# Two gates begun instead of one, weights in two parts, a new hand-written order for the second half, and other places for the third half's attention pieces

## The chip, the core and the metric

The kernel runs on one core of one Trainium2 chip. The metric is device time in microseconds (us) of one execution; the median of several runs counts. The engines are named as in the profile: PE (TensorE, matrix products), PEld (its weight loads), DVE (VectorE), ACT (ScalarE), POOL (GpSimd, which also issues the loads that change type on the way), SP (SyncE, which issues the other transfers).

## The reference

Attention with a sliding window and a few global keys, then a gated feed-forward layer:

```python
# q, k, v: (4 batches, 8 heads, 768 tokens, 64); n_global = 8, n_local = 96
scores = scale * q @ k.T                        # per batch and head
keep = (key < n_global) | ((0 <= rel) & (rel < n_local))      # rel = query - key
dist = n_local where a key is global and not local, else |rel|
scores = where(keep, scores - slope[head] * dist, -1e9)
a = softmax(scores); x = a @ v                  # -> (3072 tokens, 512)
gate = maximum(x @ w_gate, 0); val = x @ w_val  # 512 -> 1536
out = (gate * val) @ w_out                      # 1536 -> 512, float32
```

## The kernel before

The 4 x 768 tokens are cut into 8 halves of 384 tokens, numbered 0 to 7. For each half there is attention (four head pairs p = 0 to 3) and a feed-forward part. Feed-forward for half c is made of pieces: for each of 12 column blocks fc a gate piece (four products of 128x128 weights with 128x384 of xT, then a relu on ACT) and a val piece (four products, then a multiplication with the relu's result on DVE), and after that the output pieces. The four products of a piece run over the four chunks of xT, and chunk p of xT is what the normalisation of head pair p writes. Output rows n = 0, 1 are made by a seven-product scheme (m1 to m7, `winograd`) that needs sums of ht and of w_out blocks on DVE (`add`, L535; `wo_sum`), the rest by plain pieces (`outp`).

All engines run their instructions in the order in which the program was written out. That order is hand-made:

- The first half's attention runs alone. Meanwhile POOL issues loads in this order: v of half 0, the first weight group (wg[0] and wv[0], blocks fc 0 to 3), then q and k of half 1 (`kq1`, heads 4 to 7 first, then heads 0 to 3), v rows of half 1, the second weight group (fc 4 to 7).
- The second half's stage then interleaves half 1's attention with fc 0 to 7 of half 0's feed-forward. Its order is a string of short names (L802): g and v are a gate or val piece, K the transposes of q and k of a head pair, S its scores with masks (S31 is pair 3, group 1), A its sums and values, N its normalisation, m a mask built on ACT. Just before the string runs `begin()`, which starts gate 0 and val 0 with the first three of their four chunks, so that `g0` and `v0` in the string only add the last chunk. PSUM has two `ff` banks for feed-forward pieces here, two score tiles (`s`) of two banks each and two `t` banks. The piece K0 also issues q and k loads of half 2 on SP, the piece S20 the third weight group, w_out and pad fills on POOL.
- From then on `weave` mixes feed-forward pieces with attention pieces of the next half: each attention piece gets a place, a share of the stage's total weight (`spread` puts a list evenly between two shares), and is written out once the feed-forward pieces before it reach that share. PSUM now has three `ff` banks and five `x` banks. For half 2 (the third) the stage is fc 8 to 11 of halves 0 and 1 followed by their output pieces, 39 pieces of equal weight; the attention pieces of half 2 come from `attention_pieces(2)`, in which `gap` is an empty place. Its scores take four x banks for a pair, the values one for each head, and the norm (`piece_norm`, L446) frees the latter.
- At the end of that stage stood the last norm of half 2, after all other pieces. Half 2's own feed-forward then started with `begin()`, which there also begins gate 1.
- `held` (L842) is a one-element copy on POOL that reads w_out; behind it stand the last cast and the three transposing transfers for half 2's keys and queries.

Of the kernel before, what the change touches and what calls it, by code (L numbers as in the profile page):

```python
# [8 lines left out]
FP32 = mybir.dt.float32  # L9
# [6 lines left out]
def kernel(  # L16
# [19 lines left out]
    N_DC = DM // 128  # L36
# [38 lines left out]
    psum = {}  # L75
# [17 lines left out]
    GW = 4  # L93
# [399 lines left out]
    def attention_pieces(s):  # L493
        QK = lambda p: [(0.15, lambda g=g: piece_qk(s, p, g)) for g in range(3)]
        AV = lambda p: [(0.29, lambda e=e: piece_av(s, p, e)) for e in range(2)]
        N = lambda p: [(0.0, lambda: piece_norm(s, p))]
        g = QK(3)
        a = AV(2)
        gap = [(0.0, lambda: None)]
        return (QK(0) + QK(1) + AV(0) + N(0) + gap + QK(2) + AV(1) + N(1) + gap  # L500
                + g[0:1] + a[0:1] + g[1:2] + a[1:2] + g[2:3] + N(2) + AV(3) + N(3))

# [95 lines left out]
    def ffn_pieces(c):  # L598
        ht = ht_pool.tile([128, N_FC, QH], BF16, name="ht")
        st = {}  # L600

        def product(w, key, fc, d0, d1):
            key = key, fc
            if d0 == 0:
                st[key] = psum["ff"].tile([128, 512], FP32, name="ff_ps")
            for dc in range(d0, d1):
                nc.tensor.matmul(st[key][:, 0:QH], lhsT=w_of(w, dc, fc), rhs=xT_of[c][:, dc, :],  # L607
                                 start=(dc == 0), stop=(dc == N_DC - 1))

        def gate(fc, d0=0):  # L610
            product(wg, "g", fc, d0, N_DC)
            psg = st["g", fc]
            gr = gr_pool.tile([128, QH], BF16, name="grelu")
            nc.scalar.activation(gr, psg[:, 0:QH], AF.Relu, bias=0.0, scale=1.0)  # L614
            st["gr", fc] = gr

        def val(fc, d0=0):
            product(wv, "v", fc, d0, N_DC)
            psv = st["v", fc]
            nc.vector.tensor_tensor(ht[:, fc, :], psv[:, 0:QH], st["gr", fc], op=ALU.mult)  # L620

        def outp(n, part):
            if part == 0:
                st["o"] = psum["ff"].tile([128, 512], FP32, name="ff_ps")
            ps2 = st["o"]
            for fc in range(part * N_FC // 4, (part + 1) * N_FC // 4):
                nc.tensor.matmul(ps2, lhsT=ht[:, fc, n * 128 : (n + 1) * 128],  # L627
                                 rhs=wo_sb[:, fc, :],
                                 start=(fc == 0), stop=(fc == N_FC - 1))
            if part == 3:  # L630
                osb = late["osb"].tile([128, DM], FP32, name="osb")
                nc.scalar.copy(osb, ps2)
                nc.sync.dma_start(out=out_v[c, n], in_=osb)

        def begin():
            for d0, d1 in ((0, 2), (2, N_DC - 1)):
                product(wg, "g", 0, d0, d1)
                product(wv, "v", 0, d0, d1)
            if c == 2:
                product(wg, "g", 1, 0, N_DC - 1)  # L640

        plain = range(NN) if c < 1 else () if c - c % 2 in PAIRED else (NN - 1,)
        add, products = winograd([(c, ht, 0), (c, ht, 1)], "sums", (1, 5, 6, 4, 7, 2, 3) if c == NHALF - 1 else
                                 (1, 2, 5, 6, 4, 3, 7) if c in PAIRED else (1, 5, 4, 6, 2, 3, 7))
        behind = {2: [lambda: add(3, 0, 3)], 5: [lambda: add(3, 3, 6)], 8: [lambda: add(1, 0, 3)],
                  9: [lambda: add(2, 0, 3)], 10: [lambda: add(4, 0, 3)]}
        rest = tuple(lambda j=j: add(j, 3, 6) for j in (1, 2, 4))
        if c in PAIRED:
            third_of[c] = ht
        elif c - 1 in PAIRED:  # L650
            add3, products3 = winograd([(c, ht, NN - 1), (c - 1, third_of[c - 1], NN - 1)], "sums3",
                                       (1, 5, 4, 6, 2, 3, 7))
            behind.update({1: [lambda: add3(1)], 6: [lambda: add3(2)], 7: [lambda: add3(3)]})
            rest = (lambda: add3(4),) + rest

        def val_and_sums(fc):
            val(fc)
            for f in behind.get(fc, ()):
                f()

        begin_of[c] = (begin, lambda: gate(0, N_DC - 1), lambda: val(0, N_DC - 1))
        f1 = []
        for fc in range(N_FC):
            f1.append((0.65, lambda fc=fc: gate(fc)))
            f1.append((0.65, lambda fc=fc: (val if c < 1 else val_and_sums)(fc)))
        f2 = [(0.65, lambda n=n, part=part: outp(n, part))
              for n in plain for part in range(4)]
        if c == 2:
            f1[:2] = [(1.5, begin_of[c][0]), (0.15, begin_of[c][1]), (0.15, begin_of[c][2])]
            f1[3] = (0.15, lambda: gate(1, N_DC - 1))  # L670
        if c >= 1:
            f2 += (products3 if c - 1 in PAIRED else []) + products
            places = (2, 3, 5) if plain else (0, 1, 2) if c in PAIRED else (0, 1, 2, 3)
            for at, f in list(zip(places, rest))[::-1]:
                f2.insert(at, (0.0, f))
        return f1, f2
# [44 lines left out]
    scores(0, 0, 0)  # L721
    first_keys(1, A)
    nc.gpsimd.tensor_copy(hold[1], kT[0][1][0:1, 0, 0:1])
    load_w(wg[0], moe_w_gate, 0, GW * 128)
    load_w(wv[0], moe_w_val, 0, GW * 128)
    make_sel(1)
    make_sel(2)
    scores(0, 0, 1)
# [5 lines left out]
    for h0 in (4, 0):  # L734
        for i, src in enumerate((k, q)):
            nc.gpsimd.dma_start(out=kq1[:, i, h0 : h0 + 4, :], in_=rows_of(src, 1, h0, h0 + 4))
    nc.gpsimd.memset(vbuf[0][:, NT - 1, :].bitcast(mybir.dt.uint32), 0)
    for p in range(HP):
        nc.gpsimd.memset(kT[0][p][:, 6, NG + 48 : 128].bitcast(mybir.dt.uint32), 0)
# [39 lines left out]
    stack = open_psum(ff=2, s=2, t=2)  # L779
    f1_0, f2_0 = ffn_pieces(0)  # L780
    f1_1, f2_1 = ffn_pieces(1)
    g_of = [begin_of[0][1]] + [f for _, f in f1_0[2::2]]
    v_of = [begin_of[0][2]] + [f for _, f in f1_0[3::2]]
    K = [lambda p=p: second_keys(p) for p in range(HP)]

    def Z():
# [12 lines left out]

    more = {"K0": lambda: load_qk_after(2), "S20": loads}  # L800
    begin_of[0][0]()
    for f in ("m1 g0 m3 v0 m2 g1 K3 K2 m0 g3 K1 S30 S31 g2 K0 S20 v3 S11 v1 S21 A3 N3 v2 S00 S01 "  # L802
              "g5 A2 S10 g4 g6 A0 N2 v5 v4 N0 A1 N1 g7 v7 v6").split():
        i = int(f[1])
        if f[0] == "S":
            SC(i, int(f[2]))
# [35 lines left out]
    for f in (*casts[:7], lambda: nc.gpsimd.tensor_copy(held, wo_sb[0:1, N_FC - 1, 0:1]),  # L842
# [3 lines left out]
    load_v_half(3)  # L846
    weave(f1_1[G[0]])
    weave(f1_1[G[1]], [(0.1 + 0.12 * j, lambda j=j: fill_ones(nc.vector, 0, j)) for j in range(NT)])
    pieces = spread(attention_pieces(2), 0.375, 0.9)

    weave(f1_0[G[2]] + f1_1[G[2]] + f2_0 + f2_1 + [(0.0, pieces.pop()[1])],
          [(0.33, order_k[2]), (0.38, order_k[3])],
          pieces, spread(early_pieces(3), 0.58, 0.88),
          spread([(0.0, lambda j=j, part=part: wo_sum(j, part)) for j in (1, 3, 2, 4) for part in range(2)],
                 0.1, 0.74))

# [55 lines left out]
```

## Time and profile before

| | |
|---|---|
| median of 3 runs | 240.94 us (240.68 to 241.03) |
| profiled execution, its own time | 241.08 us |
| its span in the profile | 239.3 us |
| granted PE clock | 1.0 |
| PE busy | 232.4 us, 97% of the span |
| DVE, ACT, POOL busy | 172.3, 156.4, 86.0 us |

The span runs from the first to the last instruction of the program; 1.8 us of the execution lie around it. In the profile's lines, L607 is a product of a gate or val piece, L614 the relu, L620 the multiplication, L272 the transposes of K, L341 the scores S, L459 the sums and values A of the second half, L397 and L427 the scores and values of later halves, L436 and L441 the logarithm and exponential that make a reciprocal, L446 the norm, L549 the seven-product scheme. A timeline line has start, length, engine, line, operation, out<-in, shapes, count, and in brackets the idle time before it and what ended it. Products are pipelined: a product of 384 columns is listed with 0.32 us, though the next one can start after about half of that.

### The profile page before, as it was taken

What the parts mean: (1) busy time and instruction counts of PE and PEld (TensorE: products, weight loads), DVE (VectorE), ACT (ScalarE), POOL (GpSimd) and SP (SyncE); (2) the same over time, 40 slices, a digit from 0 to 9 for tenths busy, and PEclk for the clock granted to TensorE, in tenths of its full rate; (3) what the DMA queues carried; (4) which work ended last, traced back from release to release, by engine and by line L of the source; (5) the groups of instructions that cost most, each with busy time, mean ns of one, the idle gap of its engine ahead of it and who ended that gap; (6) DMA issues with size and microseconds to landing.
All of it is one profiled execution on the core that took longest, in us unless ns stands there. A gap on an engine that the chain in (4) does not pass through costs nothing.

```text
span 239.3 us, 5430 instructions
## 1 busy us (share of the span) xinstructions
PE 232.4 (97%) x1977; PEld 150.2 (63%) x1981; DVE 172.3 (72%) x456; ACT 156.4 (65%) x358; POOL 86.0 (36%) x202
## 2 busy tenths in 40 slices
PE   7999999999999999999999999999999999999994
PEld 3655555665458456676657666766678666766683
DVE  7775955858665788756787686967986786955752
ACT  5897883337776677757877578657786678634331
POOL 6776894207323952702357042723350000000000
PEclk9999999999999999999999999999999999999999
DMA  6999999994947997469439966197432200020022
GB/s 208 179 197 177 257 243 213 184 162 96 272 137 135 287 173 126 31 140 277 77 58 79 223 199 114 22 174 230 77 58 88 90 0 0 4 88 0 3 76 101
DMA packets 69460, 31.42 MB, mean 131 GB/s; under 512 B 47145, under 2 KB 66345, under 8 KB 69433
## 3 DMA queue, kind: packets, MB, share of 16 engines
q0 software_dynamic: 31744, 8.71, 35.6%
q1 hardware_dynamic: 36472, 21.45, 34.4%
q10 hardware_dynamic: 1216, 0.92, 1.2%
q8 instruction: 15, 0.25, 0.4%
q14 instruction: 13, 0.10, 0.1%
HBM read 28.41 MB, written 6.29 MB: 145 GB/s over the span
## 4 chain that ended last, share of the span: by engine, by line
PE 92%; DVE 3%; ACT 2%; DMA 1%; issue 0%
PE ff_ps L607 52%; PE ff_ps L549 12%; PE x_ps L427 6%; PE ff_ps L627 6%; PE x_ps L549 5%; PE x_ps L397 4%; PE t_ps L459 2%; PE s_ps L341 2%; PE t_ps L272 2%; DMA kq<-in_k_dram 1%; PE t_ps L310 1%; DVE xT L446 1%; ACT lnd L436 1%; PE s_ps L321 1%; ACT ef L347 0%
## 5 line engine op out<-in xcount | busy, mean ns | idle before, releaser
L607 PE MATMUL ff_ps<-xT,wg 128*128 128x384 bf16 x384 | 79.0, 326 | 0.8 <-ACT grelu L614 0.4
L607 PE MATMUL ff_ps<-xT,wv 128*128 128x384 bf16 x384 | 78.6, 326 | 0.0
L614 ACT ACTIVATE grelu<-ff_ps 128x384 bf16<-128x384 f32 x96 | 46.9, 490 | 46.6 <-PE ff_ps L607 24.5
L620 DVE TENSOR_TENSOR ht<-ff_ps,grelu 128x384 bf16<-128x384 f32 x96 | 53.2, 555 | 29.1 <-PE ff_ps L607 18.5
L607 PEld LDWEIGHTS <-wg 128*128 128x128 bf16 x384 | 36.1, 98 | 23.5 <-issue 1.0
L607 PEld LDWEIGHTS <-wv 128*128 128x128 bf16 x384 | 35.7, 98 | 23.9 <-issue 1.2
L406 ACT ACTIVATE es<-x_ps 128x360 bf16<-128x360 f32 (+2 forms) x96 | 35.8, 447 | 3.1 <-PE x_ps L397 3.0
L359 DVE TENSOR_TENSOR es<-es,m_all 128x432 bf16<-128x432 bf16 (+4 forms) x108 | 30.0, 328 | 6.0 <-ACT es L406 5.9
L446 DVE TENSOR_TENSOR xT<-x_ps,rcp 64x384 bf16<-64x384 f32 x48 | 26.6, 554 | 7.5 <-ACT rcp L441 6.8
L436 ACT ACTIVATE lnd<-x_ps 64x384 f32<-64x384 f32 x48 | 23.3, 485 | 11.3 <-PE x_ps L427 10.6
L363 POOL CAST kqc<-ks 128x384 bf16<-128x384 f32 x24 | 11.2, 514 | 33.0 <-DMA ks<-in_k_dram 33.0
L549 PEld LDWEIGHTS <-s 128*128 128x128 bf16 x216 | 21.1, 98 | 2.4
L137 POOL DMA_DIRECT2D vbuf<-in_v_dram x25 | 21.6, 876 | 1.1 <-DMA wv<-in_moe_w_val_dram 0.8
L427 PE MATMUL x_ps<-es,vbuf 128*128 128x216 bf16 (+4 forms) x216 | 21.8, 225 | 0.0
L549 PE MATMUL ff_ps<-t,s 128*128 128x256 bf16 x162 | 21.6, 273 | 0.0
L427 PEld LDWEIGHTS <-vbuf 128*128 128x128 bf16 x216 | 15.8, 97 | 6.8
L627 PE MATMUL ff_ps<-wo_sb,ht 128*128 128x512 bf16 x68 | 17.8, 379 | 0.2
L549 PEld LDWEIGHTS <-ht 128*128 128x128 bf16 x162 | 15.5, 98 | 2.5 <-DVE xT L446 0.2
L263 POOL COPY kT<-kqT 128x240 bf16<-128x240 bf16 x16 | 6.9, 431 | 23.5 <-DMA kqT<-kqc 20.7
L363 POOL CAST kqc<-qs 128x384 bf16<-128x384 f32 x24 | 12.1, 543 | 8.3 <-DMA qs<-in_q_dram 8.3
L535 DVE TENSOR_TENSOR s<-ht 128x384 bf16<-128x384 bf16 (+1 forms) x32 | 13.3, 416 | 0.9
L441 ACT ACTIVATE rcp<-lnd 128x384 f32<-128x384 f32 x24 | 12.6, 524 | 0.8
(114 smaller groups left out, 241.2 us busy)
## 6 DMA issues: line engine op xcount, KB each, us to landing
out_dram<-osb SPq DMA_DIRECT2D x23, 256.0 KB, 2.3
ks<-in_k_dram SPq DMA_DIRECT2D x6, 768.0 KB, 5.4
qs<-in_q_dram SPq DMA_DIRECT2D x6, 768.0 KB, 11.3
vbuf<-in_v_dram POOLq DMA_DIRECT2D x21, 120.0 KB, 7.7
wg<-in_moe_w_gate_dram POOLq DMA_DIRECT2D x3, 512.0 KB, 8.2
wv<-in_moe_w_val_dram POOLq DMA_DIRECT2D x3, 512.0 KB, 10.0
wo_sb<-in_moe_w_out_dram POOLq DMA_DIRECT2D x1, 1536.0 KB, 19.6
kq<-in_k_dram SPq DMA_DIRECT2D x2, 192.0 KB, 3.9
```

Of the source, the lines that this page charges most:

```text
L137: nc.gpsimd.dma_start(out=v_dst(b, NG + r0, NG + r0 + n, j), in_=v[b, :, KT * j + r0 : KT * j + r0 + n, :].rearrange("h p d -> p h d"))
L359: nc.vector.tensor_mul(for_all, for_all, mk)
L363: nc.gpsimd.tensor_copy(kqc[:, :, i].rearrange("t n (h d) -> t h n d", d=D)[:, 2 * p : 2 * p + 2], of[s][:, 2 * p : 2 * p + 2, :].rearrang ...
L406: nc.scalar.activation(es[:, e, 0:c], banks[e][:, 0:c], AF.Exp, bias=0.0, scale=scale)
L427: nc.tensor.matmul(av3[:, :, a : a + w], lhsT=vb[:, j, z0 : z0 + 128], rhs=es[:, e, c : c + NN * w].rearrange("k (n p) -> k n p", n=NN), s ...
L436: nc.scalar.activation(ln[o0 : o0 + 64], av[d0 : d0 + 64, 0:QH], AF.Ln, bias=0.0, scale=1.0)
L446: nc.vector.tensor_tensor(xT_of[s][r, p, :], av_of[s, p, e][r, 0:QH], av_of[s, p, "r"][r], op=ALU.mult)
L549: nc.tensor.matmul(st[key][:, 0:D2], lhsT=left(i), rhs=right(i), start=start and i == 0, stop=i == N2 - 1, skip_group_check=not start)
L607: nc.tensor.matmul(st[key][:, 0:QH], lhsT=w_of(w, dc, fc), rhs=xT_of[c][:, dc, :], start=(dc == 0), stop=(dc == N_DC - 1))
L614: nc.scalar.activation(gr, psg[:, 0:QH], AF.Relu, bias=0.0, scale=1.0)
L620: nc.vector.tensor_tensor(ht[:, fc, :], psv[:, 0:QH], st["gr", fc], op=ALU.mult)
L627: nc.tensor.matmul(ps2, lhsT=ht[:, fc, n * 128 : (n + 1) * 128], rhs=wo_sb[:, fc, :], start=(fc == 0), stop=(fc == N_FC - 1))
```

## The change

- `begin()` takes a score tile and puts gate 1 and val 1 of half 0 there; it starts gate 0, gate 1, val 0 and val 1 with three of their four chunks. It is no longer used for half 2, whose pieces now run plainly in order.
- The first weight group's load is cut in two: fc 0 and 1 where the whole was, fc 2 and 3 between the two pairs of `kq1` loads.
- The order string of the second half's stage is a new one, with `g1` and `v1` now only adding their last chunk.
- For half 2, each gap in the attention list is two empty places instead of one, the list is spread to 0.925 instead of 0.9, and the last norm is a member of the list instead of standing at the end.
- In half 2's feed-forward the sum `add(3, 3, 6)` stands behind val 7 instead of val 5.

```diff
@@ attention_pieces
-        gap = [(0.0, lambda: None)]
+        gap = [(0.0, lambda: None)] * (2 if s == 2 else 1)
@@ ffn_pieces, product
-            if d0 == 0:
+            if d0 == 0 and key not in st:
                 st[key] = psum["ff"].tile([128, 512], FP32, name="ff_ps")
@@ ffn_pieces, begin
         def begin():
+            two = psum["s"].tile([128, 2, 512], FP32, name="s_ps")
+            st["g", 1], st["v", 1] = two[:, 0], two[:, 1]
             for d0, d1 in ((0, 2), (2, N_DC - 1)):
-                product(wg, "g", 0, d0, d1)
-                product(wv, "v", 0, d0, d1)
-            if c == 2:
-                product(wg, "g", 1, 0, N_DC - 1)
+                for key, w in (("g", wg), ("v", wv)):
+                    for fc in range(2):
+                        product(w, key, fc, d0, d1)
@@ ffn_pieces
-        behind = {2: [lambda: add(3, 0, 3)], 5: [lambda: add(3, 3, 6)], 8: [lambda: add(1, 0, 3)],
+        behind = {2: [lambda: add(3, 0, 3)], 7 if c == 2 else 5: [lambda: add(3, 3, 6)], 8: [lambda: add(1, 0, 3)],
-        begin_of[c] = (begin, lambda: gate(0, N_DC - 1), lambda: val(0, N_DC - 1))
+        begin_of[c] = (begin, lambda fc=0: gate(fc, N_DC - 1), lambda fc=0: val(fc, N_DC - 1))
-        if c == 2:
-            f1[:2] = [(1.5, begin_of[c][0]), (0.15, begin_of[c][1]), (0.15, begin_of[c][2])]
-            f1[3] = (0.15, lambda: gate(1, N_DC - 1))
@@ loads of the first half
-    load_w(wg[0], moe_w_gate, 0, GW * 128)
-    load_w(wv[0], moe_w_val, 0, GW * 128)
+    def load_w_first(f0, f1):
+        load_w(wg[0][:, :, f0:f1], moe_w_gate, f0, f1)
+        load_w(wv[0][:, :, f0:f1], moe_w_val, f0, f1)
+
+    load_w_first(0, 256)
@@
     for h0 in (4, 0):
         for i, src in enumerate((k, q)):
             nc.gpsimd.dma_start(out=kq1[:, i, h0 : h0 + 4, :], in_=rows_of(src, 1, h0, h0 + 4))
+        if h0:
+            load_w_first(256, GW * 128)
@@ second half's stage
-    g_of = [begin_of[0][1]] + [f for _, f in f1_0[2::2]]
-    v_of = [begin_of[0][2]] + [f for _, f in f1_0[3::2]]
+    g_of = [lambda fc=fc: begin_of[0][1](fc) for fc in range(2)] + [f for _, f in f1_0[4::2]]
+    v_of = [lambda fc=fc: begin_of[0][2](fc) for fc in range(2)] + [f for _, f in f1_0[5::2]]
-    for f in ("m1 g0 m3 v0 m2 g1 K3 K2 m0 g3 K1 S30 S31 g2 K0 S20 v3 S11 v1 S21 A3 N3 v2 S00 S01 "
-              "g5 A2 S10 g4 g6 A0 N2 v5 v4 N0 A1 N1 g7 v7 v6").split():
+    for f in ("m0 g0 g1 v0 m3 K3 m2 g2 m1 v1 K2 v2 S30 K0 S31 K1 S21 g3 S20 v3 S01 A3 N3 S00 S11 "
+              "g6 g7 A2 S10 g4 v7 A0 N2 v4 v6 A1 N0 N1 g5 v5").split():
@@ third half's stage
-    pieces = spread(attention_pieces(2), 0.375, 0.9)
-
-    weave(f1_0[G[2]] + f1_1[G[2]] + f2_0 + f2_1 + [(0.0, pieces.pop()[1])],
+    weave(f1_0[G[2]] + f1_1[G[2]] + f2_0 + f2_1,
           [(0.33, order_k[2]), (0.38, order_k[3])],
-          pieces, spread(early_pieces(3), 0.58, 0.88),
+          spread(attention_pieces(2), 0.375, 0.925), spread(early_pieces(3), 0.58, 0.88),
```

## The prediction

> **What bounds the kernel now.** I read the page first, then the chain of waits in order of time, then single stretches of the timeline by engine, then the issues of transfers with their times to landing.
>
> ```profile
> PE 232.4 (97%) x1977; PEld 150.2 (63%) x1981; DVE 172.3 (72%) x456; ACT 156.4 (65%) x358; POOL 86.0 (36%) x202
> ...
> PE 92%; DVE 3%; ACT 2%; DMA 1%; issue 0%
> ```
>
> The matrix engine (PE) is the bound: 92% of the chain is its own work. What an edit can win is only the few places where the chain leaves PE, or where PE does something slower than need be. The chain (start, length, what) gives those places and the prices of PE's pieces:
>
> ```profile
> 18.99 0.50 ACT grelu L614
> 19.53 0.81 PE ff_ps L607 x4
> ...
> 28.17 0.76 PE ff_ps L607 x4
> ...
> 34.23 23.09 PE ff_ps L607 x140
> ...
> 59.09 0.38 PE x_ps L397 x8
> ...
> 73.25 0.54 PE x_ps L427 x8
> 73.79 0.66 PE x_ps L549 x6
> ...
> 79.59 0.41 PE x_ps L397 x10
> ```
>
> 140 products of 384 columns in 23.09 us are 0.165 us each. Four of them alone between two other kinds of work take 0.76, so 0.10 more than 0.66: each change between the array's shapes (transposes and denominators 128*64, scores 64*128, products 128*128) costs about 0.10. From 19.53 to 57 the chain is PE without a break, so in the second half's stage only its head, up to 20.27, has waits to give; the rest has only shape changes.
>
> **The head of the second half's stage.** PE alone:
>
> ```profile
> 17.36 0.67 PE L607 MATMUL ff_ps<-xT,wg 128*128 128x384 bf16 x2
> 17.87 0.49 PE L607 MATMUL ff_ps<-xT,wv 128*128 128x384 bf16 x2
> ...
> 20.27 0.86 PE L272 MATMUL t_ps<-ident,kq 128*64 128x128 bf16 x24
> ```
>
> From 17.36 to the first transposes (K3) at 20.27 are 2.91 us. Twelve products are 1.98, one shape change 0.10, so 0.83 is idle. Two products that should take 0.49 take 0.67: the second waits 0.18 for the second head pair's xT. That stays, since the new order begins with the same two. The other 0.65 goes: it is the wait for xT's last chunk and, most of it, g1's wait until g0's relu (18.99, 0.50) gives its bank back, as only two ff banks are open. After the change g1 and v1 lie in a score tile. Ahead of K3 are then 12 begun products and three last chunks: 15 x 0.165 + 0.18 + 0.10 = 2.75, with three products more done (0.50). Gain 2.91 + 0.50 - 2.75 = 0.66. Covers: the last xT chunk is wanted six products (1.0 us) later than the fourth's end was in the old order; g2's bank (g0's relu) has K3's transposes in front of it. Without that cover it would cost what is missing of one relu, at most 0.50.
>
> Shape changes from K3 to the stage's last product, counted in the lists (g and v are one shape, K and A another, S the third): 22 before, 23 after, so +0.10. Net -0.56.
>
> What the new order could bring in: between a K and the first S that reads its keys (two VectorE (DVE) copies, then GpSimd (POOL) copies) the old list had at least K2, g3, K1 (K3 to S30) and no wait. The shortest in the new one is K2 to S21 with v2, S30, K0, S31, K1, which is longer. S31 waits for the begun tile, so for v1's multiplication; K2, v2, S30, K0 lie between, and behind S31 all of PE would stand. The closest ff bank is v3's, wanted by g7 with S01, A3, S00, S11, g6 between, while v3's multiplication is queued on DVE behind the masks; if DVE is late there I price it at 0.1 to 0.4. ACT makes masks 0, 3, 2, 1 in other places; none is read before the S pieces.
>
> **The transfers.** POOL issues the loads:
>
> ```profile
> 7.92 0.77 POOL L155 DMA_DIRECT2D wg<-in_moe_w_gate_dram  x1
> 8.68 0.75 POOL L155 DMA_DIRECT2D wv<-in_moe_w_val_dram  x1
> ...
> 11.60 0.79 POOL L736 DMA_DIRECT2D kq<-in_q_dram  x1
> ...
> 18.31 0.79 POOL L155 DMA_DIRECT2D wg<-in_moe_w_gate_dram  x1 [1.00 <-DMA kq<-in_k_dram]
> ```
>
> The issues by window say when these four landed after their start:
>
> ```profile
> wg<-in_moe_w_gate_dram POOLq DMA_DIRECT2D x1, 512.0 KB, 5.6
> wv<-in_moe_w_val_dram POOLq DMA_DIRECT2D x1, 512.0 KB, 7.4
> kq<-in_q_dram POOLq DMA_DIRECT2D x1, 192.0 KB, 9.4
> wg<-in_moe_w_gate_dram POOLq DMA_DIRECT2D x1, 512.0 KB, 8.2
> ```
>
> So 13.5, 16.1, 21.0 and 26.5: the queue works in order, and is never empty here. Two loads become four; POOL pays 2 x 0.77 more to issue, which delays only pad fills and v loads that would queue anyway, and its next weight issue waits, as at 18.31, for the transfer eight back, now a second part. K3's POOL copies stand behind that. A half part at the whole one's rate (512 KB in 2.6) takes 1.3; at the rate of the four kq1 loads (768 KB in 4.9) it takes 1.6. Its rows (512 bytes, by the code) lie between theirs (384 and 1,024), so a part costs 0 to 0.3 more, and the queue behind all four is late by d = 0 to 1.3; I take 0.6.
>
> Who notices: the second weight group, landing at 26.5. In the kernel before its first reader is g5, the 28.17 of the chain. In the new list g6 comes first, with the same K, A and S pieces ahead but 0.75 of a four-product piece less (0.50), the 0.16 of K3 and one shape change more: 28.17 - 0.50 - 0.16 + 0.10 = 27.6. Cover 1.1, so d = 0.6 is hidden. And the third half's keys:
>
> ```profile
> 47.08 0.18 POOL L842 COPY held<-wo_sb 1x1 bf16<-1x1 bf16 x1 [4.51 <-DMA wo_sb<-in_moe_w_out_dram]
> ...
> 54.98 0.23 POOL L261 COPY kT<-kT 128x56 bf16<-128x56 bf16 x1
> ...
> 57.24 0.45 PE L397 MATMUL x_ps<-kqT,kT 64*128 64x216 bf16 x8
> ```
>
> wo_sb's landing starts the chain of SP's transposing transfers and POOL's key copies; the first scores want them 2.0 after they are there, 1.4 with PE earlier. d fits in that. The second half's q and k loads are issued from K0's place, which moves by less than a piece.
>
> The Trainium skill, "DMA: Bandwidth & Descriptors", section on the anatomy of one DMA, prices a GpSimd-issued transfer at a fixed 2.0 us plus its bytes; read as a toll in series, two more transfers would make d 4.0. The rows speak against a toll in series: four kq1 loads landed in 4.9.
>
> **The third half.** The scores of its third and fourth pair stop half way, as four x banks of five are wanted and the norm before still reads two:
>
> ```profile
> 63.29 0.79 PE L397 MATMUL x_ps<-kqT,kT 64*128 64x216 bf16 x8
> 64.02 0.39 PE L627 MATMUL ff_ps<-wo_sb,ht 128*128 128x512 bf16 x1
> ...
> 68.55 0.79 PE L397 MATMUL x_ps<-kqT,kT 64*128 64x216 bf16 x8
> ```
>
> 0.73 instead of 0.38, so 0.35, twice. The places: 39 items of equal weight, old spacing 0.525 x 39 / 26 = 0.79, new 0.55 x 39 / 28 = 0.77 of an item. The values stay behind items 21 and 27, the scores go from 23 to 24 and from 29 to 30: one product more (0.65) between, which covers 0.35. The last values go from item 34 to 35, the last norm from the end (39) to 36. Before, PE waits for that norm in the next half's begun gates:
>
> ```profile
> 77.92 0.65 PE L607 MATMUL ff_ps<-xT,wg 128*128 128x384 bf16 x3
> 78.95 0.32 PE L607 MATMUL ff_ps<-xT,wg 128*128 128x384 bf16 x1 [0.38 <-DVE xT L446]
> ```
>
> Three products from 77.92 end at 78.41; the next starts 0.54 later. With the norm two pieces sooner that goes. Last, in the next half:
>
> ```profile
> 88.32 0.40 PE L397 MATMUL x_ps<-kqT,kT 64*128 64x216 bf16 x7
> 88.99 0.32 PE L397 MATMUL x_ps<-kqT,kT 64*128 64x192 bf16 x3 [0.27 <-DVE xT L446]
> 89.25 0.34 PE L607 MATMUL ff_ps<-xT,wg 128*128 128x384 bf16 x1
> ```
>
> 0.93 instead of 0.41: 0.52, behind a norm that itself stands behind add(3, 3, 6) (L535, just ahead of it on DVE). The change moves that sum two products later; the norm then starts earlier by about its length. Removed in all: 0.35 + 0.35 + 0.54 + 0.52 = 1.76.
>
> What is late next: the last values now stand behind m4, so on ACT and DVE their work meets that of the last products.
>
> ```profile
> 73.84 0.99 ACT L436 ACTIVATE lnd<-x_ps 64x384 f32<-64x384 f32 x2
> 74.87 0.52 ACT L441 ACTIVATE rcp<-lnd 128x384 f32<-128x384 f32 x1
> 75.30 0.35 ACT L578 COPY osb<-x_ps 128x256 f32<-128x256 f32 x1
> 75.55 0.38 ACT L584 COPY osb<-ff_ps 128x256 f32<-128x256 f32 x1
> ```
>
> The norm on DVE and the additions of m2, m3, m7:
>
> ```profile
> 77.45 0.41 DVE L589 TENSOR_TENSOR osb<-ff_ps,osb 128x256 f32<-128x256 f32 x1
> 77.78 1.11 DVE L446 TENSOR_TENSOR xT<-x_ps,rcp 64x384 bf16<-64x384 f32 x2
> ```
>
> From the values' start (0): PE has them done at 0.54, m6 1.20, m2 1.86, m3 2.52, m7 3.18, g0 3.84. ACT: m4's copy to 0.55, logarithms to 1.54, reciprocal to 2.1, m6's copy to 2.5; m7 writes that bank and wants it at 2.52, so 0 to 0.25. DVE: norm 2.1 to 3.2, then four additions, 0.35 to 0.41 apart, to 3.6, 4.0, 4.4 and 4.8. v0 takes m3's bank: wanted at 3.84, free at 4.0, 0.2 to 0.35. g1 takes m7's: 0.05 to 0.15. The values themselves start one item closer to their last masks: 0.1. Sum 0.35 to 0.85; I take 0.75, near the upper end, since each crosses three queues. Without begin(), which started three products ahead of the norm, g0's last chunk is wanted at 3.7, the norm done at 3.2: hidden.
>
> **Sum.** -0.56 - 1.76 + 0.75 = -1.57. From 57 on PE is the chain to the end, so this stays. The profiled execution took 241.08, so 239.5; the median of the runs is 240.94, 0.14 lower, so 239.4.
>
> **Rivals.**
> First: the second half's new order makes its own waits. DVE late at g7 (0.4) and d at its upper end (1.3: 0.2 at g6) eat the 0.56: -1.0 or so, 239.9. For it: the cover at g6 shrinks from 1.6 to 1.1. Against: the old order had no wait after 20.27 with a similar load.
> Second: the third half's waits only change place. If v0, g1, m7 and the values wait as long together as the 1.76 that goes, -0.56 stays: 240.4. For it: m2, m3, m7 and the norm share one DVE queue, and the sum above needs four small margins. Against: two of the removed waits (0.35 each) lie before that place.
> Third, slower: a part costs by its number of rows. A half has the same rows as a whole, so 2.6 instead of 1.3, d = 5.2. The second weight group lands at 31.7, g6 waits 4.1; the third half's keys are then late by less than PE. -1.57 + 4.1 = +2.5, 243.4. It turns slower once d passes 1.1 + 1.57 = 2.7, a part at 1.95. Against: four kq1 loads, each with as many rows as a part, took 1.2 each.
> Fourth: a fixed toll in series of 2.0 for each transfer, d = 4.0: -1.57 + 2.9 = +1.3, 242.2. The rows above speak against it; it is the rule of the Trainium skill's page named there.
> Fifth: the change does little of what it says, as the banks come free no sooner: 240.9.
>
> **How the numbers follow.** Chances: forecast 0.55, first 0.17, second 0.14, third 0.08, fourth 0.03, fifth 0.03. A measurement can tell about 0.2%, 0.48 us, from no change, so faster means below 240.46. Faster: the forecast, 0.15 of the first, 0.05 of the second: 0.75. Same: 0.06 of the second, the fifth and 0.01 of the first: 0.10. Slower: 0.15. The range starts at 238.8 (new waits 0.35, a norm in the next half sooner still) and ends at 241.2, which takes in the first, second and fifth and leaves out the third, the fourth and the ends of the others, together about 0.2.
>
> **What would show it.** K3's transposes at about 20.1 and no relu in the chain ahead of them; g6 at 27.6 and the stage's end about 0.6 sooner; the second wg landing at 26.5 to 27.8; eight-product score groups of the third half at 0.38; no wait for L446 in the next half's first gate, but up to 0.35 ahead of its first val; no wait at the third pair's scores after that. Wrong, if PE waits for wg or wv, for a POOL key copy, or if the next half's first gates start no sooner than 76.0.

## The result, and the profile after

| | before | changed |
|---|---|---|
| median of 6 runs each | 240.99 us (240.68 to 241.28) | 239.65 us (239.12 to 240.18) |
| ratio | | 0.995, 95% interval 0.9935 to 0.9966 |
| profiled execution, its span | 241.08, 239.3 us | 240.08, 238.3 us |

The changed kernel is 0.8 to 1.6 us faster (1 minus the ratio's bounds, of 241); 239.4 was predicted. In a second comparison it was 239.99 against 240.64, ratio 0.9962 (0.9943 to 0.9981); times of one kernel differ by up to 2 us from one execution to another, so that single profiles are compared by their places, not by their ends. The profiled execution shown here is 0.43 slower than the median of its kernel, so the traces differ by 1.00 only; where that goes is told below.

The page of the changed kernel, busy times and chain:

```profile
PE 231.7 (97%) x1977; PEld 150.1 (63%) x1981; DVE 171.8 (72%) x456; ACT 156.1 (66%) x358; POOL 89.5 (38%) x204
...
PE 86%; DMA 7%; DVE 2%; POOL 1%; ACT 1%; issue 1%; DVEq 0%
```

PE's own share of the chain fell from 92% to 86% while the kernel became faster, and DMA came in with 7%. That does not mean that 7% is lost: the chain followed back from the end now crosses, at one point, to a load that landed last. The chain in order of time shows where:

```profile
10.81 7.24 DMA wg<-in_moe_w_gate_dram
...
18.34 9.37 DMA wg<-in_moe_w_gate_dram
27.71 0.05 issue
27.75 1.47 PE ff_ps L607 x8
```

10.81 is the second part of the first group's gate half; POOL waits for its landing (18.05) before it issues the load at 18.34, the second weight group's gate half. 27.75 is g6, its first reader. PE was busy nearly all the time while that load was under way; the loss is only what PE stood still ahead of 27.75. The timeline of PE, head of the second half's stage and g6:

```profile
17.30 0.67 PE L607 MATMUL ff_ps<-xT,wg 128*128 128x384 bf16 x2
...
19.75 0.33 PE L607 MATMUL ff_ps<-xT,wv 128*128 128x384 bf16 x1
20.01 0.53 PE L272 MATMUL t_ps<-ident,kq 128*64 128x128 bf16 x12
...
27.06 0.52 PE L341 MATMUL s_ps<-kqT,kT 64*128 64x216 bf16 x10
27.75 1.47 PE L607 MATMUL ff_ps<-xT,wg 128*128 128x384 bf16 x8 [0.18 <-DMA wg<-in_moe_w_gate_dram]
```

K3 starts at 20.01 with three more products done than at 20.27 before: the wait for g0's relu and for xT's last chunk is gone. But from the ten scores to g6 are 0.69. In a later kernel, whose g6 waits for nothing, the same stretch is 0.45, so 0.24 here is the load.

The third half and the start of the next, PE:

```profile
63.45 0.45 PE L397 MATMUL x_ps<-kqT,kT 64*128 64x216 bf16 x8
63.83 1.47 PE L627 MATMUL ff_ps<-wo_sb,ht 128*128 128x512 bf16 x5
...
72.56 0.71 PE L427 MATMUL x_ps<-es,vbuf 128*128 128x216 bf16 x8
73.22 0.81 PE L549 MATMUL ff_ps<-t,s 128*128 128x256 bf16 x6
...
74.53 0.82 PE L549 MATMUL ff_ps<-wo_sb,s 128*128 128x256 bf16 x6
75.60 0.81 PE L549 MATMUL ff_ps<-t,s 128*128 128x256 bf16 x6 [0.26 <-ACT osb L584]
76.25 0.81 PE L607 MATMUL ff_ps<-xT,wg 128*128 128x384 bf16 x4
77.31 0.49 PE L607 MATMUL ff_ps<-xT,wv 128*128 128x384 bf16 x2 [0.24 <-DVE osb L574]
...
87.51 0.48 PE L397 MATMUL x_ps<-kqT,kT 64*128 64x216 bf16 x10
87.92 0.82 PE L607 MATMUL ff_ps<-xT,wg 128*128 128x384 bf16 x4
```

Scores now take 0.38 (63.45 to 63.83) where they took 0.73, the gate at 76.25 no longer stops for a norm, and the scores at 87.51 take 0.41 where they took 0.93. New are the last values (0.66 in place of 0.54), m7 (75.60: 1.07 after m3 in place of 0.65, for ACT's copy out of its bank) and the first val (77.31: 1.06 after the gate in place of 0.65, for an addition on DVE).

How far PE is ahead of the kernel before, at the same piece of work: 0.48 at the third half's first scores (56.76, before 57.24), 0.82 at 79.12, 1.33 from 87.92 on, and 1.00 from 170.26 to the end. Of the 0.48, 0.06 is there before the new order begins: the second half's first product is at 17.30 in this execution and at 17.36 in the one before. The last step back is a wait that the kernel before did not have in its profile:

```profile
169.27 0.81 PE L607 MATMUL ff_ps<-xT,wv 128*128 128x384 bf16 x4
170.26 0.81 PE L607 MATMUL ff_ps<-xT,wg 128*128 128x384 bf16 x4 [0.17 <-DVE ht L620]
```

Four products, but 0.99 to the next in place of 0.65: 0.34, for a multiplication on DVE.

### The profile page after: what moved, and what is told of

Read it like the earlier page. It is cut to its first block, busy times and chain, and to the rows that moved or that the text cites. A ratio compares the mean times of both kernels' runs of the same rounds, so it can differ in the third digit from the quotient of the medians.

```text
span 238.3 us, 5431 instructions
## 1 busy us (share of the span) xinstructions
PE 231.7 (97%) x1977; PEld 150.1 (63%) x1981; DVE 171.8 (72%) x456; ACT 156.1 (66%) x358; POOL 89.5 (38%) x204
## 4 chain that ended last, share of the span: by engine, by line
PE 86%; DMA 7%; DVE 2%; POOL 1%; ACT 1%; issue 1%; DVEq 0%
PE ff_ps L607 50%; PE ff_ps L549 12%; DMA wg<-in_moe_w_gate_dram 7%; PE ff_ps L627 7%; PE x_ps L427 6%; PE x_ps L549 5%; PE x_ps L397 4%; PE t_ps L700 1%; PE t_ps L459 1%; POOL kq L737 1%; PE t_ps L272 1%; DVE es L359 0%; DVE ht L620 0%; ACT lnd L436 0%; DVE osb L574 0%
## 5 line engine op out<-in xcount | busy, mean ns | idle before, releaser
L607 PE MATMUL ff_ps<-xT,wg 128*128 128x384 bf16 x380 | 77.7, 326 | 0.4 <-DMA wg<-in_moe_w_gate_dram 0.2
L607 PE MATMUL ff_ps<-xT,wv 128*128 128x384 bf16 x380 | 77.6, 326 | 0.2 <-DVE osb L574 0.2
L436 ACT ACTIVATE lnd<-x_ps 64x384 f32<-64x384 f32 x48 | 23.3, 485 | 10.9 <-PE x_ps L427 10.2
L363 POOL CAST kqc<-ks 128x384 bf16<-128x384 f32 x24 | 12.1, 554 | 31.7 <-DMA ks<-in_k_dram 31.7
L535 DVE TENSOR_TENSOR s<-ht 128x384 bf16<-128x384 bf16 (+1 forms) x32 | 12.5, 392 | 0.8
```

What stands on the lines that cost most here:

```text
L363: nc.gpsimd.tensor_copy(kqc[:, :, i].rearrange("t n (h d) -> t h n d", d=D)[:, 2 * p : 2 * p + 2], of[s][:, 2 * p : 2 * p + 2, :].rearrang ...
L436: nc.scalar.activation(ln[o0 : o0 + 64], av[d0 : d0 + 64, 0:QH], AF.Ln, bias=0.0, scale=1.0)
```

## Experiments

All kernels were timed in five rounds against the kernel before; those of one batch share its runs (medians 240.64, 240.69 and 240.76).

| kernel | median us | ratio to before | 95% interval |
|---|---|---|---|
| changed, again | 239.99 | 0.9962 | 0.9943 to 0.9981 |
| second half's part alone | 240.34 | 0.9983 | 0.9969 to 0.9997 |
| third half's part alone | 240.10 | 0.9975 | 0.9957 to 0.9994 |
| changed, spread to 0.90 | 239.40 | 0.9945 | 0.9925 to 0.9964 |
| changed, whole first load | 239.44 | 0.9940 | 0.9919 to 0.9962 |
| whole load, 0.90 | 238.90 | 0.9915 | 0.9894 to 0.9937 |
| whole load, K2 behind K3 | 239.25 | 0.9929 | 0.9909 to 0.9950 |
| changed, sum at val 5 | 240.05 | 0.9967 | 0.9951 to 0.9982 |
| before, split load | 240.77 | 1.0002 | 0.9990 to 1.0014 |
| changed, one gate begun | 239.98 | 0.9970 | 0.9958 to 0.9983 |
| whole load, 0.90, K2 behind K3 | 238.75 | 0.9924 | 0.9906 to 0.9943 |
| the same, A2 and S10 ahead of g6 | 240.02 | 0.9970 | 0.9954 to 0.9985 |

**The changed kernel again**, no edit.

> The changed kernel itself, beside the parts on one chip. Both theories: 1.3 us (1.0 to 1.6) shorter than the kernel before. In a new profile the first theory (the change's waits repeat, what comes late in the span is chance) expects the waits at g6 (0.25), m7 (0.42) and the next half's first val (0.40) again, and the wait of 0.33 at 169.8 us gone or elsewhere. The rival (the new order shifts POOL's casts against DVE's masks for good) expects that wait again, within 0.5 us of 170.

Measured 0.9962. Its profiled execution took 241.06, and shows what can happen at g6. PE's timeline:

```profile
26.91 0.52 PE L341 MATMUL s_ps<-kqT,kT 64*128 64x216 bf16 x10
28.26 0.50 PE L607 MATMUL ff_ps<-xT,wg 128*128 128x384 bf16 x2 [0.83 <-DMA wg<-in_moe_w_gate_dram]
...
31.93 0.82 PE L607 MATMUL ff_ps<-xT,wv 128*128 128x384 bf16 x4 [0.44 <-DMA wv<-in_moe_w_val_dram]
```

1.35 from the scores to g6, so 0.90 lost there, and 0.61 more at v7 (a gate at 30.66 takes 1.27 to the next in place of 0.66). The same kernel, the same order, another landing: 28.21 in place of 27.71. The waits at m7 and at the first val come again (0.25 and 0.24 idle in this trace). The product that waited at 170.26 waits again too, at 171.21, and loses 0.18 in place of 0.34: the rival of this run has its sign, at about half the size.

**The two parts apart.** Second half's part alone: the list, begin and split load as changed, the third half's `gap`, spread, last norm and sum as before, and for half 2 a `begin2` that starts gate 0, val 0 and gate 1 as the old `begin()` did. Shown against the changed kernel:

```diff
-        gap = [(0.0, lambda: None)] * (2 if s == 2 else 1)
+        gap = [(0.0, lambda: None)]
...
+            f1[:2] = [(1.5, begin2), (0.15, lambda: gate(0, N_DC - 1)), (0.15, lambda: val(0, N_DC - 1))]
+            f1[3] = (0.15, lambda: gate(1, N_DC - 1))
...
-    weave(f1_0[G[2]] + f1_1[G[2]] + f2_0 + f2_1,
+    pieces = spread(attention_pieces(2), 0.375, 0.9)
+
+    weave(f1_0[G[2]] + f1_1[G[2]] + f2_0 + f2_1 + [(0.0, pieces.pop()[1])],
...
-          spread(attention_pieces(2), 0.375, 0.925), spread(early_pieces(3), 0.58, 0.88),
+          pieces, spread(early_pieces(3), 0.58, 0.88),
```

> The kernel before with the second half's part of the change alone: begin with two gates in a score tile, first weights in two parts, the new order. Theory (both parts work apart): 0.4 us shorter than before, from 0.65 of idle removed at the stage's head, 0.10 for one shape change more, and 0.25 of a new wait for the second weight group at g6; first scores of the third half at about 56.8 instead of 57.24. Rival (the gain at the stage's head is lost again before the third half's scores, which wait for keys that are late with the loads): no difference, scores at 57.2.

Third half's part alone, shown against the kernel before:

```diff
-        gap = [(0.0, lambda: None)]
+        gap = [(0.0, lambda: None)] * (2 if s == 2 else 1)
...
-    weave(f1_0[G[2]] + f1_1[G[2]] + f2_0 + f2_1 + [(0.0, pieces.pop()[1])],
+    weave(f1_0[G[2]] + f1_1[G[2]] + f2_0 + f2_1,
...
-          pieces, spread(early_pieces(3), 0.58, 0.88),
+          spread(attention_pieces(2), 0.375, 0.925), spread(early_pieces(3), 0.58, 0.88),
```

with the sum behind val 7 and no begin() in half 2, as changed.

> The kernel before with the third half's part alone: two empty places at each gap, spread to 0.925 with the last norm in the list, no begun gates for the third half, add(3, 3, 6) behind val 7. Theory: 1.76 of waits go, 0.9 of new ones come at the last values, m7 and the next half's first val: 0.85 us shorter than before. Rival (the third half's waits only change place, the gain is all the second half's): within 0.3 of before.

Measured 0.9983 and 0.9975, that is -0.41 (-0.75 to -0.07) and -0.60 (-1.03 to -0.14) of 240.64. Both parts count; their sum, -1.01, is what the whole shows beside them (-0.91). PE in the kernel with the second half's part, at g6, at a score group of the third half and in the next half's begun gates:

```profile
26.58 0.52 PE L341 MATMUL s_ps<-kqT,kT 64*128 64x216 bf16 x10
27.47 0.82 PE L607 MATMUL ff_ps<-xT,wg 128*128 128x384 bf16 x4 [0.38 <-DMA wg<-in_moe_w_gate_dram]
...
62.52 0.80 PE L397 MATMUL x_ps<-kqT,kT 64*128 64x216 bf16 x8
63.24 1.04 PE L627 MATMUL ff_ps<-wo_sb,ht 128*128 128x512 bf16 x4
...
77.14 0.65 PE L607 MATMUL ff_ps<-xT,wg 128*128 128x384 bf16 x3
78.17 0.32 PE L607 MATMUL ff_ps<-xT,wg 128*128 128x384 bf16 x1 [0.38 <-DVE xT L446]
```

The third half's waits are all there again (0.72 for eight scores, 0.54 for the norm, and at 88.18 the wait for the norm ahead of the third pair's scores), so they belong to the third half's part, as the prediction had it. And 0.44 is lost at g6, most of what the head won. In the kernel with the third half's part alone the two new waits stand as in the changed one, to 0.01:

```profile
75.61 0.81 PE L549 MATMUL ff_ps<-t,s 128*128 128x256 bf16 x6 [0.26 <-ACT osb L584]
...
77.31 0.48 PE L607 MATMUL ff_ps<-xT,wv 128*128 128x384 bf16 x2 [0.23 <-DVE osb L574]
```

**The place of the last values.** All as changed, but

```diff
-          spread(attention_pieces(2), 0.375, 0.925), spread(early_pieces(3), 0.58, 0.88),
+          spread(attention_pieces(2), 0.375, 0.9), spread(early_pieces(3), 0.58, 0.88),
```

> The changed kernel with the third half's list spread to 0.90 instead of 0.925. By the places this puts the last values behind item 34 as in the kernel before, the last norm behind 35 and the scores still behind 24 and 29. Theory (the new waits at m7 and at the first val come from the last values standing behind m4, so that ACT and DVE do their work ahead of the last products' copies and additions): both waits go, 0.7 us shorter than the changed kernel, 2.0 shorter than before. Rival (they come from the norm standing ahead of the additions wherever it stands): m7 and the first val still wait together over 0.5, no change from the changed kernel.

Measured 239.40 against 239.99. PE, and POOL's last key copy ahead of the third half's first scores:

```profile
55.76 0.45 PE L397 MATMUL x_ps<-kqT,kT 64*128 64x216 bf16 x8 [0.43 <-POOL kT L261]
...
74.73 0.82 PE L549 MATMUL ff_ps<-t,s 128*128 128x256 bf16 x6
75.38 0.81 PE L607 MATMUL ff_ps<-xT,wg 128*128 128x384 bf16 x4
76.35 0.81 PE L607 MATMUL ff_ps<-xT,wv 128*128 128x384 bf16 x4 [0.16 <-DVE osb L574]
```

```profile
55.27 0.43 POOL L261 COPY kT<-kT 128x56 bf16<-128x56 bf16 x1
```

m7 (74.73) no longer waits, and the first val loses 0.32 in place of 0.40. So these waits come from the values' place, as the prediction said. By the places in the code only half of the last values went back behind item 34; the other half stayed behind 35, with the norm. In the time the gain is not told from nothing: 0.9945 and 0.9962 have intervals of 0.2% each way, and the theory's 0.7 us is neither reached nor excluded.

The edit does one thing more, which neither the expectation nor the rival had: the first scores of the third half move from behind item 16 to behind item 15 (the trace has 188 products of gate and val pieces ahead of them in place of 192). They now stand 0.65 sooner and wait 0.43 for POOL's key copies, ready at 55.70. One product later, at 55.98, they would not have waited.

**The split load.** All as changed, but the first weight group whole, where it was before:

```diff
-    load_w_first(0, 256)
+    load_w_first(0, GW * 128)
-        if h0:
-            load_w_first(256, GW * 128)
```

> The changed kernel with the first weight group loaded in one part each (512 KB), as before the change; all else as changed. Theory (the two parts delay the second weight group, and the new order wants it sooner, so its landing shows in the time): the second wg lands about 1.0 earlier than in the changed kernel run beside it, g6 waits 0 to 0.3, 0.3 us faster than the changed kernel. Rival 1 (the parts are hidden, as the prediction took them): no difference, within 0.2. Rival 2 (the early first part is needed by the second half's stage): the begin's first products wait for wg at 17.3 and the kernel is 0.3 or more slower than the changed one.

And the reverse, the kernel before with nothing but the split:

```diff
-    load_w(wg[0], moe_w_gate, 0, GW * 128)
-    load_w(wv[0], moe_w_val, 0, GW * 128)
+    load_w_first(0, 256)
...
+        if h0:
+            load_w_first(256, GW * 128)
```

> The kernel before with the first weight group in two parts, nothing else changed. Theory (the parts delay the second weight group by 0.3 to 1.2, and in the old order its first reader, g5, comes 10.8 after the second half's first product, 0.6 later than g6 in the new one): no difference, within 0.2 of the kernel before, and no wait or at most 0.2 at g5. Rival (the parts cost by themselves, in the queue or on GpSimd): 0.4 or more slower than the kernel before.

The whole load gave 239.44, ratio 0.9940 beside 0.9962. It is not slower, so the early first part gains nothing that shows. But its margin is thin: in this run's profile the whole val load landed at 18.15, and the stage's first val products, at 18.20, came 0.16 late. The kernel before with the split gave 1.0002: in the old order the split is free. Over the fourteen profiles, when the second group landed, counted from the second half's first product:

| first group | kernel: landing (wait at g6) | mean |
|---|---|---|
| whole | before 9.10 and third half's part 10.47 (old order, no wait); whole load 10.51 (0.10), with 0.90 9.20 (none), with K2 10.14 (0.20), with both 10.07 (0.14); A2 ahead of g6 9.28 (g6 later) | 9.82 |
| two parts | changed 10.41 (0.24), again 11.06 (0.90); second half's part 10.61 (0.44), 0.90 10.37 (0.21), sum at 5 10.74 (0.58), one gate 9.95 (none); split only 10.24 (old order, no wait) | 10.48 |

The parts cost 0.66 in the mean, but the landing of one and the same kind of load differs by up to 1.4 from one execution to another, so that the means of seven leave this difference uncertain by about 0.6 each way. Right behind the four weight loads, at the last `kq1` load, the parts are 0.30 later in the mean (4.61 against 4.31 after the first product), so only about half of the 0.66 arises in the queue up to there; what makes the rest is not shown. The profile of the whole load itself shows no earlier landing than the changed kernel's (10.51 against 10.41), against its expectation. g6 wants it 10.2 after the first product, g5 in the old order 10.8. So the old order held in its three profiles, and with the new one g6 waits in eight of ten, by 0.10 to 0.90; in the other two an early landing saved it.

**Both together.**

```diff
-    load_w_first(0, 256)
+    load_w_first(0, GW * 128)
...
-          spread(attention_pieces(2), 0.375, 0.925), spread(early_pieces(3), 0.58, 0.88),
+          spread(attention_pieces(2), 0.375, 0.9), spread(early_pieces(3), 0.58, 0.88),
```

> As the kernel with the whole first load, and the third half's pieces spread to 0.90 of the weave in place of 0.925. Theory (m7's wait of 0.42 and part of the wait in the next half's first val are made by the place of the last values, and the wait for the second weight group by the two parts; the two are independent): 0.6 less than the whole load alone, about 0.9 below the changed kernel, ratio to the kernel before about 0.991 to 0.993. Rival (with PE earlier it then waits for the third half's keys, 0.6 at their first scores as in the run with the spread alone, and this eats the second gain): no better than the run with the spread alone, ratio 0.9945.

Measured 238.90, 0.9915: the theory's numbers, and better than the changed kernel. The two edits were each made twice, beside the other's two settings. Whole for split: 0.9940 against 0.9962 and 0.9915 against 0.9945; 0.90 for 0.925: 0.9945 against 0.9962 and 0.9915 against 0.9940. One pair has an interval of about 0.3% each way and shows nothing by itself; the mean of two pairs, -0.26% and -0.21%, has about 0.2% (the intervals taken as independent). So each edit seems to bring something like 0.5 us, only just told from nothing; with 0.995, the changed kernel's ratio in the first comparison, in place of 0.9962 the means are -0.20% and -0.15%, and this is not told. The two together are: 0.9915 (0.9894 to 0.9937) beside 0.995 (0.9935 to 0.9966). The first scores stand one product sooner here as well, but in this execution their keys were ready at 54.75, and they start at 55.89 without a wait. The chain on its page has no load of weights left:

```profile
PE 95%; DMA 1%; DVE 1%; ACT 1%; issue 0%; DVEq 0%
```

and PE's timeline has g6 right behind the scores:

```profile
27.09 0.52 PE L341 MATMUL s_ps<-kqT,kT 64*128 64x216 bf16 x10
27.54 1.47 PE L607 MATMUL ff_ps<-xT,wg 128*128 128x384 bf16 x8
```

**Two shape changes fewer**, on the whole load, then on the whole load with 0.90:

```diff
-    for f in ("m0 g0 g1 v0 m3 K3 m2 g2 m1 v1 K2 v2 S30 ...
+    for f in ("m0 g0 g1 v0 m3 K3 K2 m2 g2 m1 v1 v2 S30 ...
```

> As the kernel with the whole first load, and in the second half's stage K2 directly behind K3, so two changes of the array's shape fewer (21 in place of 23). Theory (a change costs 0.10 of PE's time and is not covered): 0.2 faster than the whole load alone. Rival (g2 then waits for g0's relu, or the third half's keys end PE's lead): no difference, within 0.1, or slower.

> The whole first load, the third half's pieces spread to 0.90, and K2 directly behind K3, all three together. Theory (independent terms, 0.55, 0.55 and 0.2 as measured one at a time): 238.7, ratio to the kernel before 0.9905. Rival (with PE 0.2 earlier again it waits at g6 for the second weight group or at the third half's first scores for their keys): no better than without K2 moved, 0.9915 or above.

0.9929 beside 0.9940, and 0.9924 beside 0.9915: no difference that can be told. PE does save what the theory says: from K3 to the ten scores ahead of g6 it takes 6.82 in the first's profile (19.93 to 26.75), and 7.05 with K2 in its old place (20.04 to 27.09), so 0.23 for two changes. But then it loses 0.20 at g6 in the first and 0.14 in the second, which also waits 0.15 at the third half's first scores. There the rival stands: PE comes sooner and waits for the same load.

**The second gate begun.** All as changed, but begin() without the score tile, and K3 as cover for the relu:

```diff
-            two = psum["s"].tile([128, 2, 512], FP32, name="s_ps")
-            st["g", 1], st["v", 1] = two[:, 0], two[:, 1]
...
-    for f in ("m0 g0 g1 v0 m3 K3 m2 g2 m1 v1 K2 v2 S30 ...
+    for f in ("m0 g0 v0 m3 K3 m2 g1 m1 v1 K2 g2 v2 S30 ...
```

> The changed kernel without the score tile in the begin: it starts one gate and value, so 6 products in place of 12 ahead of the first last chunk, and the list begins m0 g0 v0 m3 K3 m2 g1 m1 v1 K2 g2 v2, so that K3 stands ahead of g1; all behind as changed. Theory (the score tile only lifts the wait for g0's relu and for xT's last chunk, and K3 covers the first of them; xT's last chunk is then wanted six products sooner): 0 to 0.4 slower than the changed kernel, ratio to the kernel before 0.996 to 0.998. Rival (the begun second gate is what brings the stage's gain): 0.6 or more slower, ratio 0.9985 or above.

Measured 0.9970, beside 0.9962 and 0.995 of the changed kernel: the rival (0.9985 or above) falls, if narrowly, as the interval ends at 0.9983. PE:

```profile
18.86 0.53 PE L272 MATMUL t_ps<-ident,kq 128*64 128x128 bf16 x12
19.35 0.81 PE L607 MATMUL ff_ps<-xT,wg 128*128 128x384 bf16 x4
...
27.51 1.48 PE L607 MATMUL ff_ps<-xT,wg 128*128 128x384 bf16 x8
```

g1 at 19.35 does not wait. g6 starts 10.34 after the first product (17.17); with the score tile and no late load it is 10.21. So by this profile the score tile is worth 0.13 beyond that, and K3 between g0 and g1 removes the relu's wait as well.

**The sum.** All as changed, but

```diff
-        behind = {..., 7 if c == 2 else 5: [lambda: add(3, 3, 6)], ...
+        behind = {..., 5: [lambda: add(3, 3, 6)], ...
```

> The changed kernel with the half's sum add(3, 3, 6) put back behind val 5, where it was before the change; all else as changed. Theory (this sum stood ahead of the norm on DVE, and the third pair's scores in the next half waited 0.5 for it): the wait near 88 comes back, 0.3 to 0.5 slower than the changed kernel. Rival (the wait goes because PE reaches the place differently, or is taken up by the later wait near 170): no difference, within 0.15.

Measured 0.9967 beside 0.9962, the rival's number. PE at the third pair's scores:

```profile
87.65 0.67 PE L397 MATMUL x_ps<-kqT,kT 64*128 64x216 bf16 x10
88.25 0.82 PE L607 MATMUL ff_ps<-xT,wg 128*128 128x384 bf16 x4
```

0.60, where it is 0.41 in the changed kernel and 0.93 before. The sum's move takes 0.19; the other 0.33 go with the rest of the third half's part, as the kernel with the second half's part alone still waits there. 0.19 is less than this comparison can tell (about 0.3%, 0.7 us).

**A later first reader.** On the whole load, 0.90 and K2 behind K3:

```diff
-              "g6 g7 A2 S10 g4 v7 A0 N2 v4 v6 A1 N0 N1 g5 v5").split():
+              "A2 S10 g6 g7 g4 v7 A0 N2 v4 v6 A1 N0 N1 g5 v5").split():
```

> As the kernel with all three together, and in the second half's stage A2 and S10 moved ahead of g6 and g7: the second weight group's first reader comes 0.8 later, and there is one change of the array's shape fewer. Theory (the landing of this group, 9.1 to 11.1 after the stage's first product from one execution to another, decides the wait at g6): no wait at g6, 0.2 to 0.4 faster than with g6 first, and the times lie closer together. Rival (S01, S00, S11 and S10 now follow each other too closely for ScalarE, which frees their two score tiles): a wait of 0.5 or more in front of S10, no gain or slower.

1.3 slower than without it, 240.02 against 238.75. A new wait, though not the one that the rival named. PE, and DVE in the same stretch:

```profile
27.37 0.50 PE L459 MATMUL t_ps<-ef,ones 128*64 128x216 bf16 x10
28.76 0.50 PE L459 MATMUL t_ps<-ef,vbuf 128*64 128x216 bf16 x10 [0.89 <-DVE xT L487]
```

```profile
25.84 1.41 DVE L359 TENSOR_TENSOR ef<-ef,m_all 128x384 bf16<-128x384 bf16 x5
27.18 0.54 DVE L620 TENSOR_TENSOR ht<-ff_ps,grelu 128x384 bf16<-128x384 f32 x1
27.65 0.58 DVE L359 TENSOR_TENSOR ef<-ef,m_all 128x384 bf16<-128x384 bf16 x2
28.16 0.54 DVE L487 TENSOR_TENSOR xT<-t_ps,rcp 128x384 bf16<-128x384 f32 x1
```

A2's values need a t bank that pair 3's norm (L487) still reads, and that norm stands in DVE's queue behind seven masks and a multiplication. g6 and g7 had been the cover of that: 1.05 from 27.71 to 28.76.

## Why the prediction was right, and where it was not

**The head** was right to 0.1: K3 at 20.01 (predicted 20.1), no relu in front. The reason given, that the banks of the score tile lift the wait, is one way to lift it and not the only one: the kernel with one gate begun shows that K3 as cover is enough but for 0.13. The fifth rival, banks that come free no sooner, falls with this.

**The transfers** are the step that failed. The size agrees: d was taken as 0.6, and the fourteen landings have 0.66 in the mean, give or take 0.6. Wrong was "Cover 1.1, so d = 0.6 is hidden". The cover was counted from 26.46, the landing in one profile, 9.10 after the stage's first product, and this was the earliest of all fourteen. Against the mean of the whole loads (9.82) g6 has 0.4, less than d. The first rival had this wait, with 0.2; it was 0.24, 0.90, 0.44, 0.21 and 0.58 in five of the six profiles with the parts and this reader. The third and fourth rival fall: a part by its rows would have put the group 5.2 later, and two tolls in series 4.0; 0.66 was measured. The Trainium skill's fixed cost, "DMA: Bandwidth & Descriptors", section on the anatomy of one DMA, is therefore not a toll in series for queued transfers here.

**w_out and the third half's keys** were given 1.4 of cover, again from one landing (47.03). It landed between 46.7 and 49.05 in the others. In the changed kernel the landing was 47.41, the keys were ready at 56.20 and the first scores start at 56.76: no wait, but 0.56 of cover in place of 1.4. Two kernels did wait there, and not for a late landing (46.90 and 47.44): both have the spread of 0.90, which puts these scores one product sooner.

**The third half.** The removed waits were right one by one: 0.35, 0.35, 0.54 and 0.52 are gone, 1.76. Of the last, 0.33 was put down to the wrong edit, the sum. The new waits were named rightly but too small: 0.75 taken and 0.85 the upper end, 0.94 measured. m7 has 0.42 in place of 0 to 0.25, v0 0.40 in place of 0.2 to 0.35, the values 0.12 in place of 0.1, g1 nothing. The mis-sized term is m7: the prediction had ACT's copy done 2.5 after the values' start and PE there at 2.52; the trace has PE there at 2.62 (75.18) and m7 released by that copy (L584) at 3.04 (75.60). ACT's queue was half a microsecond longer than summed. In the changed kernel it reads:

```profile
73.33 0.39 ACT L578 COPY osb<-x_ps 128x256 f32<-128x256 f32 x1
73.74 0.99 ACT L436 ACTIVATE lnd<-x_ps 64x384 f32<-64x384 f32 x2
...
75.20 0.35 ACT L584 COPY osb<-ff_ps 128x256 f32<-128x256 f32 x1
```

The sum had m4's copy (L578) done 0.55 after the values' start at 72.56; it is done 1.16 after (73.72). Ahead of it stand the reciprocal of the pair before, which ends at 72.91, and the copies of m1 and m5, and the sum left these out. The norm, and with it the additions that the first val waits for, are late by as much: the norm was put at 2.1 to 3.2 after the values' start and ran from 2.77 to 3.91.

The lead that PE gains over this stretch is 0.85 (0.48 to 1.33); 1.01 was predicted. The second rival, waits that only change place, falls: the third half's part alone is faster.

**The sum.** -1.57 was predicted. In the profile: the head and stage -0.48 (predicted -0.56; the load at g6 takes 0.24 of the gain, and 0.06 is the stage's earlier start), the third half -0.85 (-1.01), the wait near 170 +0.34 (not seen), together about -1.00. By the medians -1.34 (-0.8 to -1.6), in the second comparison -0.9 (-1.4 to -0.5). The way and the main terms were right. That the first median came within 0.25 us of the forecast is in part luck: the second is 0.6 off, and the profile shows two waits, at g6 and near 170, that the sum put at nothing.

**The wait near 170** stays half open. It was in seven of the fourteen profiles, 0.16 to 0.52, in kernels with and without each part of the change, so no one edit of it makes the wait. It goes with how far DVE's masks meet POOL's casts (last section): in the five profiles in which the masks just ahead of that place take 0.6 longer than alone, PE loses 0.18 to 0.52; in the six with 0.3 longer it loses 0.16 in two and nothing in four; in the three with nothing longer, nothing. No run removed the casts, so this is read from traces and not shown by an experiment.

## What to carry to other kernels

A cover counted from a single profile's landing holds for that execution only: look at several profiles of the same loads before a reader is moved up, and keep the spread, here 1.4 us, as a margin. Where work of another kind can stand behind a producer (K3 between g0 and g1), it hides the wait almost as well as a further bank does (to 0.13 us here). When a spread of places is changed, work out every place: 0.90 for 0.925 moved not only the last values but also the first scores, into a wait. And test the parts of a combined change singly: here one of them, the split load, gained nothing that a run shows, and leaving it out with the values slightly sooner gave 0.9915 in place of 0.995.

## What the runs showed of the hardware

A queue of loads issued by POOL lands at its own pace from one execution to another. The first of the weight loads, issued at 7.3 to 7.9 as one part, landed between 13.46 and 15.04, and the second group's 9.1 to 10.5 after the stage's first product, in kernels whose loads are the same up to there.

DVE's masks and POOL's casts take longer where they run at the same time. The changed kernel's timeline beside the wait near 170, two masks of DVE singly and then four casts of POOL:

```profile
168.15 0.68 DVE L359 TENSOR_TENSOR es<-es,m_all 128x432 bf16<-128x432 bf16 x1
...
168.75 0.48 DVE L359 TENSOR_TENSOR es<-es,m_all 128x48 bf16<-128x48 bf16 x1
```

```profile
166.86 2.34 POOL L363 CAST kqc<-qs 128x384 bf16<-128x384 f32 x4 [0.44 <-DMA qs<-in_q_dram]
```

The same two masks at 161.68 and 161.97, with no cast running, take 0.37 and 0.18. The casts, taken singly, are 0.51, 0.51, 0.83 and 0.65. This is no chance of one place: from the third half on, over the fourteen profiles, the masks of 48 elements take 0.17 to 0.18 where no POOL work runs (137 of them) and 0.48 beside a cast (all 12), and casts take 0.50 to 0.56 apart from masks and sums and up to 0.92 beside them. The Trainium skill, "SBUF — State Buffer", section "SBUF: two separate sides", says that an operation of DVE with two SBUF inputs and one of GpSimd that reads SBUF lock a shared port pair, the other waiting the whole time. The 0.3 that each mask loses agrees with that, as does the longer cast; no run here takes the casts away, and none shows by which path the two meet.
